# Sliding-window attention and SwiGLU on one Trainium2 core: a fence read moved from ScalarE to VectorE, and an eviction moved from VectorE to ScalarE

## The chip, the cores and the metric

The kernel runs on one core of a Trainium2 chip. Its time is the device time of one execution in microseconds. The core has five engines that run side by side, each with its own queue in program order: TensorE (PE in the profile; PEld is its weight loads), VectorE (DVE), ScalarE (ACT), GpSimd (POOL) and SyncE (SP, which issues DMAs). They wait for one another through semaphores.

## The reference

Causal attention with a window of 64 positions over 8 batches of 8 heads (576 positions, head size 64), then a gated feed-forward block over all 4608 tokens.

```python
scores = scale * np.matmul(q, k.transpose(0, 1, 3, 2))
rel = pos[:, None] - pos[None, :]
mask = (rel >= 0) & (rel < window)
...
attn = attn / (np.sum(attn, axis=-1, keepdims=True) + 1e-09)
return np.matmul(attn, v).astype(np.float32)
...
g = x @ w_gate
silu = g * (1.0 / (1.0 + np.exp(-g)))
val = x @ w_val
return (silu * val @ w_out).astype(np.float32)
```

The output of attention, as 4608 rows of 512, is `x`; `w_gate` and `w_val` are 512x1536, `w_out` is 1536x512.

## The kernel before

**Tiling.** The tokens go in nine steps, t = 0 to 8, of 512 tokens each: eight hold the first 512 positions of a batch, and step 7 (`LAST`) gathers the last 64 positions of all eight. The weights stay in SBUF as bf16. A step needs attention (scores, exponentials, masks, totals, mixing with v, division by the totals), the gate and value products with SiLU into `hT` (12 groups of 128 rows), and the projection with `w_out` into four groups of 128 tokens.

**Order.** The order of each engine's instructions is the order in which the program writes them; nothing reorders them. The loop over t from 1 (line 749) interleaves two steps: between the gate stage of step t-1 and that of step t, TensorE works on the attention of t and, between its pieces, on the projection of t-1. For t from 2 to 8 this stretch is, with line numbers of the kernel before:

1. `set_exp` (751): ScalarE loads the table with exp and ln. `scores(t, 0)` (752): 32 score matmuls in 64x64 quadrants of the array into the banks `two[0]` and `two[1]`, one for each h of two heads; then for each h an exponential on ScalarE (line 283) into `eb`, and on VectorE the product with the mask (286) and the sum `both` of two halves (291).
2. `project_quads(..., range(12), 0)` (753): the first half of the projection of token groups 0 and 2, in quadrants, into banks 5 and 7. The two row halves of the array (x = 0 and 1) work for different groups here, and swap groups in the second half.
3. The fence (754 to 757, and `marker(6, 1)` in 761). `marker` (367) is a matmul of 16 columns in one row half, into a bank that holds nothing. Two of them follow the first half of the projection, one in each row half. ScalarE reads one word of each of their banks into `seen`. A third marker, behind the scores of step 4, writes the second bank again and so waits for that read. Since TensorE's queue is in order, the second half of the projection starts behind it, and the two row halves cannot meet in one bank.
4. `scores(t, 1)` (760): the same as in 1 for the other two head pairs. Its matmuls write `two[0]` and `two[1]` again, so they wait for ScalarE's exponentials of step 1.
5. The second half of the quadrant projection (762, 764) with the totals of the first half of the heads between (`sums`, 763: matmuls of line 303, logarithms of line 317), then the mixing with v (766, line 381).
6. Group 0 is evicted by ScalarE (767); the totals of the other heads follow (768); `end()` inverts the totals by exp(-ln) on ScalarE (320). Group 2 is evicted by VectorE (771). Twelve matmuls project token group 1 into bank 5 (772, line 449).
7. `scale_all` (773): four products on VectorE (397) give `xT` of step t. `project_end(t - 1, 1, bank[5])` (774): VectorE copies group 1 from bank 5 to SBUF (line 469) and SP issues its four stores (488). Twelve matmuls project group 3 into bank 4 (775).
8. `set_silu` (776): ScalarE loads the SiLU table. VectorE evicts group 3 from bank 4 (778). POOL waits for `xT` with a one-column copy (779), casts v and issues loads for step t+2.
9. Twelve rounds of `gate_value` (794): eight matmuls (440) of 512 columns into a gate bank and a value bank, SiLU on ScalarE (433), product on VectorE (434). The gate bank alternates between banks 5 and 4 beginning with 5, the value bank between 7 and 6. Four rounds are followed by transposes of q and k of the next step on VectorE (208, 218).

Of the kernel before, what the change touches and what calls it, by code (L numbers as in the profile page):

```python
# [11 lines left out]
AF = mybir.ActivationFunctionType  # L12
# [5 lines left out]
def kernel(  # L18
# [10 lines left out]
    nc = tc.nc  # L29
    S, D, H = 576, 64, 8  # L30
# [15 lines left out]
    bank = [two[i][:, j] for i in range(2) for j in range(2)]  # L46
# [10 lines left out]
    eb = [cst.tile([P, 17, 64], BF16, name=f"eb{i}") for i in range(4)]  # L57
# [4 lines left out]
    seen = cst.tile([D, 1], FP32, name="seen")  # L62
# [3 lines left out]
    def batch(t):  # L66
        return t if t < LAST else t - 1

    def blocks(ap, t, lo, hi):

        e = 4 if t < TURNED else 16
        w = 64 // e
        return ap.rearrange("r (e x) -> r e x", e=e)[:, :, w * lo:w * hi]
# [176 lines left out]
    def half(x):  # L250
        return slice(64 * x, 64 * x + 64)

    def scores(t, w):

        qT = queries[t]
        s_ps = two[0], two[1]
        for j in range(8):
            if t == LAST:
                k_j = kT[t % 2 if j < 4 else 2]
                pieces = [(j, j + 1, 0, k_j, P * (j % 4) + 64),  # L260
                          (j, j + 1, 1, k_j, P * (j % 4))]
            else:
                pieces = [(j, min(8, j + 2), 0, kT[t % 2], 64 * j)]
            for lo, hi, c, src, k0 in pieces:
                for h in range(2):
                    for x in range(2):
                        slot = s_ps[h][half(x)].rearrange("r a b -> r (a b)")
                        n = hi - lo
                        o = P * j + 64 * c
                        nc.tensor.matmul(  # L270
                            slot[:, o:o + 64 * n].rearrange(
                                "r (n e y) -> r e n y", n=n, e=16
                            ),
                            src[half(h), 2 * w + x, k0:k0 + 64],
                            blocks(qT[half(h), 2 * w + x], t, lo, hi).rearrange(
                                "r e (n y) -> r e n y", n=n
                            ),
                        )
        n = 1024 if t == LAST else 960
        for h in range(2):  # L280
            E = eb[2 * w + h]
            flat = E[:].rearrange("r s z -> r (s z)")[:, 64:64 + n]
            nc.scalar.activation(  # L283
                flat, s_ps[h][:].rearrange("r a b -> r (a b)")[:, 0:n], AF.Exp, scale=0.125
            )
            nc.vector.tensor_mul(  # L286
                flat, flat, mask[:].rearrange("r j c e y -> r (j c e y)")[:, 0:n]
            )
            both = epool.tile([P, 8, 64], BF16, name="both", tag="both")
            lo = 2 if t == LAST else 0  # L290
            nc.vector.tensor_add(both[:], E[:, 1:17:2], E[:, lo:lo + 15:2])  # L291
            weights[t, w, h] = E, both

    def totals_first(u, d_ps):
        for h in range(2):
            nc.tensor.matmul(
                d_ps[half(h)], ones[:, 0:D], weights[0, u][:, h, :]
            )
# [71 lines left out]
    def mix(t, w, o):  # L370
        E = [weights[t, w, h][0] for h in range(2)]
        for j in range(8) if t == LAST else (0, 2, 4, 6, 1, 3, 5, 7):
            if t == LAST:
                pieces = [(j, j + 1, 2 * j + 1 + c, vl[:, j, 1 - c]) for c in range(2)]
            else:
                pieces = [(j, min(8, j + 2), 2 * j + 1, vb[t % 2][:, j])]
            for lo, hi, s0, src in pieces:
                n = hi - lo
                for h in range(2):
                    for x in range(2):  # L380
                        nc.tensor.matmul(  # L381
                            blocks(o[x][half(h)], t, lo, hi).rearrange(
                                "r e (n y) -> r n e y", n=n
                            ),
                            src[half(x), w, h],
                            E[h][half(x), s0:s0 + n].rearrange("r n (e y) -> r n e y", e=16),
                            start=lo == 0 and s0 == 1, stop=lo == 7 and (t != LAST or s0 == 16),
                        )
# [16 lines left out]
    def d_tile():  # L405
        return bank[6 + take("v")]
# [60 lines left out]
    def project_end(t, s, o_ps, copy=nc.vector.tensor_copy):  # L467
        os_ = fsb.tile([P, 512], FP32, name="os_", tag="os_", bufs=4)
        copy(os_[:], o_ps[:])
        rows = out[S * batch(t):S * batch(t) + 512]  # L470
        if t < TURNED or t == NT - 1:
            if t < TURNED:
                rows = rows.rearrange("(r e) f -> e r f", e=4)[s]
            else:
                rows = rows[P * s:P * s + P]
            if t < TURNED or s == 0:
                for i in range(2):
                    nc.sync.dma_start(rows[half(i)], os_[half(i)])
            else:
                nc.sync.dma_start(rows, os_[:])  # L480
            return
        if t == LAST:
            rows = out.rearrange("(b s) f -> b s f", s=S)[:, 512:S]
            rows = rows.rearrange("b (r e) f -> e b r f", e=16)
        else:
            rows = rows.rearrange("(r e) f -> e r f", e=16)
        for i in range(4):
            nc.sync.dma_start(rows[4 * s + i], os_[32 * i:32 * i + 32])

    def out_tile():  # L490
        return bank[4 + take("g")]
# [72 lines left out]
    on_v, on_p, on_a = nc.vector.tensor_copy, nc.gpsimd.tensor_copy, nc.scalar.copy  # L564
# [14 lines left out]
    def weigh_first(u):  # L579
        E = eb[u][:, 1:17].rearrange("r (h y) z -> r h (y z)", h=2)  # L580
        nc.scalar.activation(E, two[u % 2][:], AF.Exp, scale=0.125)
        weights[0, u] = E
# [134 lines left out]
    second_halves(1, hi, 0, on_v)  # L717
    for u in (2, 3):
        turn_q(1, u)
    scores(1, 0)  # L720
    tiles = [out_tile(), d_tile(), out_tile(), d_tile()]

    def columns(c0, c1, s0=0, s1=4):
        project_part(0, range(s0, s1), tiles[s0:s1], range(c0, c1))
# [1 line left out]
    columns(0, 2, 0, 2)  # L726
    columns(0, 2, 2, 4)
    columns(2, 3)
    scores(1, 1)
    columns(3, 7)  # L730
    ends = [sums(1, w, two[w:w + 1]) for w in range(2)]
    for end in ends:
# [16 lines left out]
    for t in range(1, NT):  # L749
        if t > 1:  # L750
            set_exp()
            scores(t, 0)
            project_quads(t - 1, tiles, range(12), 0)
            for x in range(2):
                marker(4 + 2 * x, x)
            for x in range(2):
                on_a(seen[:], bank[4 + 2 * x][0:D, 0:1])
            if t == 2:
                stage_v(3)
            scores(t, 1)  # L760
            marker(6, 1)
            project_quads(t - 1, tiles, range(7), 1)
            end = sums(t, 0, two[0:1])
            project_quads(t - 1, tiles, range(7, 12), 1)
            for w in range(2):
                mix_half(t, w, two[1 - w])
            project_end(t - 1, 0, tiles[0], on_a)
            ends = end, sums(t, 1, (bank[4], bank[6]))
            for end in ends:
                end()  # L770
            project_end(t - 1, 2, tiles[2])
            project_part(t - 1, (1,), (bank[5],), range(12))
            scale_all(t, (two[1], two[0]))
            project_end(t - 1, 1, bank[5])
            project_part(t - 1, (3,), (bank[4],), range(12))
        set_silu()
        if t > 1:
            project_end(t - 1, 3, bank[4], on_v)
        on_p(past[:], xT[t][:, 3, 0:1])  # L779
        if t + 1 == LAST:  # L780
            load_last_v()
        elif t + 1 < NT and t > 1:
            cast_v(t + 1)
        if t + 2 < NT:
            load_qk(t + 2)
            if t > 1 and t + 2 != LAST:
                stage_v(t + 2)
        if t == 2:
            k_l = cast.tile([P, 4, 4, 4 * D], BF16, name="k_l", tag="c0")
        if t in (2, 3):  # L790
            load_k(k_l, [(b, S - P) for b in range(4, 8)], quarters[2 * t - 4:2 * t - 2])
        turns = (6, 7, 9, 10) if t == 1 else (1, 4, 7, 10)
        for m in range(12):
            gate_value(t, m)
            if m in turns and t + 1 < NT:
                turn(t + 1, turns.index(m))
            if (t, m) in late:
                turn_k(kT[2], k_l, late.index((t, m)))
# [32 lines left out]
```

## Time and profile before

| | us |
|---|---|
| median of three runs | 324.82 |
| the three runs | 324.44, 324.82, 325.74 |
| the profiled execution | 324.94 |
| its span in the profile | 322.8 |
| granted TensorE clock | 0.999 |
| TensorE busy | 316.8 (98%) |
| VectorE busy | 213.4 (66%) |
| ScalarE busy | 168.8 (52%) |
| one step of the loop, t=5 (gate stage to gate stage) | 33.9 |

How to read it: times in the profile count from the span's start. A line of the timeline gives start, length, engine, source line, operation, output and inputs, how many like it were joined, and in brackets how long the engine had been idle and what ended that. The ends of matmuls are modelled: each is drawn longer than its distance to the next, so a row of matmuls overlaps. Rows of weight loads (PEld) have no such overlap, and their idle times show the distance. In a group's row stand busy time, mean length in ns, and the idle time ahead of its members with what ended it.

### The profile page before, as it was taken

The page shows a single profiled execution, that of the slowest core. Times are in us where ns is not written, and L with a number is a line of the kernel's source. Part 1 is how long each engine was busy: PE and PEld are TensorE (multiplying, and loading weights), DVE is VectorE, ACT ScalarE, POOL GpSimd, SP SyncE. Part 2 cuts the span into 40 slices and gives each one's busy share as a digit, 9 for nine tenths or more (in the row PEclk, how much of TensorE's full clock was granted, in tenths as well). Part 3 has the DMA queues.
Part 4 walks back from the last instruction along what each step waited for, and adds up shares of the span by engine and source line. Part 5 has one row for each costly group of instructions (what it writes and reads, how often), then busy time and mean ns, then how long its engine had stood idle before and what let it go on. Part 6 is the DMA issues. An engine that isn't in the chain of part 4 may idle for free.

```text
span 322.8 us, 8085 instructions
## 1 busy us (share of the span) xinstructions
PE 316.8 (98%) x3299; PEld 155.0 (48%) x3299; DVE 213.4 (66%) x342; ACT 168.8 (52%) x239; POOL 146.8 (45%) x267
## 2 busy tenths in 40 slices
PE   7999999999999999999999999999999999999996
PEld 4644444445444544454445544454446444544443
DVE  4856746497676856676588666867796576854422
ACT  5954665348533863376336823583347533863310
POOL 4955666777557235751751099407856300000000
PEclk9999999999999999999999999999999999999999
DMA  7999999999699449983996269619998400011003
GB/s 250 203 196 198 206 154 226 194 200 125 131 191 197 52 100 169 199 96 73 163 196 75 67 119 120 69 31 140 189 191 107 97 18 0 5 73 60 0 19 113
DMA packets 83525, 40.42 MB, mean 125 GB/s; under 512 B 64160, under 2 KB 78752, under 8 KB 83488
## 3 DMA queue, kind: packets, MB, share of 16 engines
q0 software_dynamic: 51488, 22.59, 58.0%
q1 hardware_dynamic: 31456, 16.79, 22.7%
q8 instruction: 26, 0.43, 0.6%
q10 hardware_dynamic: 544, 0.52, 0.5%
q14 instruction: 11, 0.09, 0.1%
HBM read 53.02 MB, written 9.44 MB: 194 GB/s over the span
## 4 chain that ended last, share of the span: by engine, by line
PE 78%; DMA 15%; POOL 3%; issue 2%; DVE 1%; SPq 0%; POOLq 0%
PE one L440 46%; PE one L449 14%; PE one L461 11%; DMA wv<-in_moe_w_val_dram 3%; DMA wo<-in_moe_w_out_dram 3%; DMA q_s<-in_q_dram 2%; PE two L270 2%; DMA wg<-in_moe_w_gate_dram 2%; PE two L381 2%; DMA k_s<-in_k_dram 1%; DMA q_f<-in_q_dram 1%; DMA vb<-in_v_dram 1%; POOL vb L153 1%; PE one L502 1%; POOL v L145 1%
## 5 line engine op out<-in xcount | busy, mean ns | idle before, releaser
L433 ACT ACTIVATE sg<-one 128x512 f32<-128x512 f32 x107 | 63.9, 597 | 123.5 <-PE one L440 97.5
L434 DVE TENSOR_TENSOR hT<-sg,one 128x512 bf16<-128x512 f32 x107 | 74.0, 692 | 63.5 <-PE one L440 59.4
L440 PE MATMUL one<-xT,wg 128*128 128x512 bf16 x416 | 106.7, 379 | 0.2
L440 PE MATMUL one<-xT,wv 128*128 128x512 bf16 x416 | 106.7, 379 | 0.1
L127 POOL DMA_DIRECT2D k_s<-in_k_dram x112 | 60.4, 564 | 28.8 <-DMA q_s<-in_q_dram 15.0
L440 PEld LDWEIGHTS <-wg 128*128 128x128 bf16 x416 | 40.5, 98 | 50.1 <-issue 2.1
L440 PEld LDWEIGHTS <-wv 128*128 128x128 bf16 x416 | 40.7, 98 | 49.4 <-issue 0.4
L449 PE MATMUL one<-wo,hT 128*128 128x512 bf16 x252 | 56.5, 379 | 0.0
L779 POOL COPY past<-xT 128x1 bf16<-128x1 bf16 x8 | 1.5, 190 | 89.8 <-DVE xT L397 89.8
L461 PE MATMUL one<-wo,hT 64*64 64x512 bf16 x672 | 40.0, 377 | 0.0
L449 PEld LDWEIGHTS <-hT 128*128 128x128 bf16 x252 | 23.8, 98 | 29.3 <-issue 2.0
L218 DVE STREAM_TRANSPOSE kT<-k_s 128x512 bf16<-128x512 bf16 x28 | 36.0, 1286 | 0.5 <-DMA vb<-in_v_dram 0.5
L397 DVE TENSOR_TENSOR xT<-two,r 128x512 bf16<-128x512 f32 x34 | 21.2, 683 | 22.1 <-ACT r L320 18.1
L283 ACT ACTIVATE eb<-two 128x960 bf16<-128x960 f32 (+1 forms) x32 | 29.5, 974 | 1.7 <-PE two L270 1.2
L286 DVE TENSOR_TENSOR eb<-eb,mask 128x960 bf16<-128x960 bf16 (+1 forms) x32 | 21.0, 656 | 7.0 <-ACT eb L283 6.8
L461 PEld LDWEIGHTS <-hT 64*64 64x64 bf16 x672 | 18.4, 107 | 14.5
L208 DVE STREAM_TRANSPOSE qT<-q_s 128x512 bf16<-128x512 bf16 x32 | 22.3, 701 | 0.1
L320 ACT ACTIVATE r<-r 128x1024 f32<-128x1024 f32 (+1 forms) x20 | 18.5, 972 | 0.1
L291 DVE TENSOR_TENSOR both<-eb 128x512 bf16<-128x512 bf16 x32 | 13.6, 425 | 1.1
L153 POOL DMA_DIRECT2D vb<-in_v_dram x16 | 10.9, 687 | 6.2 <-DMA wo<-in_moe_w_out_dram 3.7
L92 POOL DMA_DIRECT2D q_s<-in_q_dram x24 | 12.9, 546 | 1.2 <-DMA v<-in_v_dram 0.8
L510 ACT ACT_TABLE_LOAD x9 | 11.5, 1283 | 2.0 <-issue 1.9
(134 smaller groups left out, 241.1 us busy)
## 6 DMA issues: line engine op xcount, KB each, us to landing
k_s<-in_k_dram POOLq DMA_DIRECT2D x112, 56.0 KB, 5.3
q_s<-in_q_dram POOLq DMA_DIRECT2D x24, 248.0 KB, 6.7
v_f<-in_v_dram SPq DMA_DIRECT2D x40, 128.0 KB
wg<-in_moe_w_gate_dram POOLq DMA_DIRECT2D x5, 256.0 KB, 8.9
wv<-in_moe_w_val_dram POOLq DMA_DIRECT2D x5, 256.0 KB, 9.0
q_f<-in_q_dram SPq DMA_DIRECT2D x4, 256.0 KB
wo<-in_moe_w_out_dram POOLq DMA_DIRECT2D x2, 512.0 KB, 10.7
vb<-in_v_dram POOLq DMA_DIRECT2D x16, 64.0 KB, 6.5
```

The source lines that it names most:

```text
L127: nc.gpsimd.dma_start(k_s[p0:p0 + 32, g, :, 0:w], k[b, a:H:2, s:s + P].rearrange("u (r e) d -> r u (e d)", e=4) [:, :, 32 * c:32 * c + w],)
L208: nc.vector.transpose(queries[t][:, u, :].rearrange("r (e x) -> r e x", e=16), staged[t][0][:, u].rearrange("r (e d) -> r e d", d=D)[:, :, ...
L218: nc.vector.transpose(dst[:, u, :].rearrange("r (g x e) -> r g e x", g=4, e=4), k_s[:, :, u].rearrange("r g (e d) -> r g e d", d=D)[:, :, ...
L283: nc.scalar.activation(flat, s_ps[h][:].rearrange("r a b -> r (a b)")[:, 0:n], AF.Exp, scale=0.125)
L286: nc.vector.tensor_mul(flat, flat, mask[:].rearrange("r j c e y -> r (j c e y)")[:, 0:n])
L320: nc.scalar.activation(r, r, AF.Exp, scale=-1.0)
L397: nc.vector.tensor_mul(x, o_ps, r)
L433: nc.scalar.activation(sg[:], g_ps[:], AF.Silu)
L434: nc.vector.tensor_mul(hT[t][:, m, :], sg[:], v_ps[:])
L440: nc.tensor.matmul(ps[:], w[:, c, P * m:P * m + P], xT[t][:, c, :], start=(c == 0), stop=(c == 3),)
L449: nc.tensor.matmul(o_ps[:], hT[t][:, c, P * s:P * s + P], wo[:, c, :], start=(c == 0), stop=(c == 11),)
L461: nc.tensor.matmul(tiles[s][half(y)], hT[t][half(x), c, r0:r0 + 64], wo[half(x), c, :], start=not back and c == 0, stop=bool(back) and c = ...
```

## The change

`scores` no longer emits the masks itself. For each h it emits the exponential and returns a function that emits mask product and sum. Where nothing else changes (step 1, and the second call of each step) these functions are called at once, and VectorE and ScalarE keep their order. In the first call of each step from t=2 on, VectorE's order becomes: product and sum for h = 0, the two reads of the fence, product and sum for h = 1. The reads leave ScalarE. And `project_end` of token group 1 (line 774 before) copies with ScalarE, which puts the copy behind the inversions and ahead of the SiLU table load.

```diff
+        return [weigh(t, w, h, s_ps[h]) for h in range(2)]
+
+    def weigh(t, w, h, s_ps):
         n = 1024 if t == LAST else 960
-        for h in range(2):
-            E = eb[2 * w + h]
-            flat = E[:].rearrange("r s z -> r (s z)")[:, 64:64 + n]
-            nc.scalar.activation(
-                flat, s_ps[h][:].rearrange("r a b -> r (a b)")[:, 0:n], AF.Exp, scale=0.125
-            )
+        E = eb[2 * w + h]
+        flat = E[:].rearrange("r s z -> r (s z)")[:, 64:64 + n]
+        nc.scalar.activation(
+            flat, s_ps[:].rearrange("r a b -> r (a b)")[:, 0:n], AF.Exp, scale=0.125
+        )
+
+        def masked():
             nc.vector.tensor_mul(
                 flat, flat, mask[:].rearrange("r j c e y -> r (j c e y)")[:, 0:n]
             )
...
             weights[t, w, h] = E, both
+
+        return masked
+
+    def ready(masks):
+        for masked in masks:
+            masked()
...
-    scores(1, 0)
+    ready(scores(1, 0))
...
-    scores(1, 1)
+    ready(scores(1, 1))
...
             set_exp()
-            scores(t, 0)
+            masks = scores(t, 0)
+            masks[0]()
             project_quads(t - 1, tiles, range(12), 0)
             for x in range(2):
                 marker(4 + 2 * x, x)
             for x in range(2):
-                on_a(seen[:], bank[4 + 2 * x][0:D, 0:1])
+                on_v(seen[:], bank[4 + 2 * x][0:D, 0:1])
+            masks[1]()
             if t == 2:
                 stage_v(3)
-            scores(t, 1)
+            ready(scores(t, 1))
             marker(6, 1)
...
             scale_all(t, (two[1], two[0]))
-            project_end(t - 1, 1, bank[5])
+            project_end(t - 1, 1, bank[5], on_a)
             project_part(t - 1, (3,), (bank[4],), range(12))
```

## The prediction

> **What bounds the kernel now.** I read the page first: busy shares, then the chain that ended last.
>
> ```profile
> span 322.8 us, 8085 instructions
> ...
> PE 316.8 (98%) x3299; PEld 155.0 (48%) x3299; DVE 213.4 (66%) x342; ACT 168.8 (52%) x239; POOL 146.8 (45%) x267
> ...
> PE 78%; DMA 15%; POOL 3%; issue 2%; DVE 1%; SPq 0%; POOLq 0%
> ```
>
> TensorE (PE) is busy in 98% of the span and carries 78% of the chain; VectorE (DVE) and ScalarE (ACT) carry next to nothing. So an edit on DVE or ACT counts only where TensorE stands still for it. A busy PE hides short stops, because the drawn tail of one matmul covers the start of the next; I therefore looked for distances between matmul starts. The chain in order of time (start, length, what) shows two short pieces of "issue" in every step of the loop; those of step t=5 are:
>
> ```profile
> 176.74 0.01 issue
> 176.76 0.17 PE one L368
> ...
> 186.11 0.04 issue
> 186.14 20.88 PE one L440 x96
> ```
>
> They stand ahead of the fence's last matmul (line 368) and of the first gate matmul (line 440), the two places that the change touches. What holds TensorE there is read from the timeline (start, length, engine, group).
>
> First the entry into the gate stage: the pitch of undisturbed matmuls, the place itself in step t=5, then one row of step t=2 and the page's group of these weight loads.
>
> ```profile
> 153.12 1.03 PE L440 MATMUL one<-xT,wv 128*128 128x512 bf16 x4
> 153.98 1.03 PE L440 MATMUL one<-xT,wg 128*128 128x512 bf16 x4
> ...
> 184.81 0.68 DVE L397 TENSOR_TENSOR xT<-two,r 128x512 bf16<-128x512 f32 x1
> 185.41 0.68 DVE L469 COPY os__2849<-one 128x512 f32<-128x512 f32 x1
> 185.73 0.10 PEld L440 LDWEIGHTS <-wg 128*128 128x128 bf16 x1
> 186.14 0.38 PE L440 MATMUL one<-xT,wg 128*128 128x512 bf16 x1
> 186.15 0.69 DVE L469 COPY os__2868<-one 128x512 f32<-128x512 f32 x1
> ...
> 84.50 0.10 PEld L440 LDWEIGHTS <-wg 128*128 128x128 bf16 x1 [0.26 <-issue]
> ...
> L440 PEld LDWEIGHTS <-wg 128*128 128x128 bf16 x416 | 40.5, 98 | 50.1 <-issue 2.1
> ```
>
> Four matmuls take 153.98 - 153.12 = 0.86 us, so the pitch is 0.215. The first gate weights are loaded at 185.73, right behind the start of the last projection matmul, and the gate matmul should start at 185.73 + 0.215 = 185.945. It starts at 186.14. DVE's eviction of token group 1 ends at 185.41 + 0.68 = 186.09, just before. The first gate tile of a step is bank 5, the bank that this eviction reads, so TensorE waits for DVE: 0.195 us here. Between two loads an ordinary idle time is 0.215 - 0.098 = 0.117; step t=2 has 0.26, so it loses 0.145. The last row sums the idle time of the weight loader where nothing but the issue ended it, once in each of the seven steps: 2.1 - 7 x 0.117 = 1.28. Six times 0.195 and 0.145 give 1.31. I take 1.3 us.
>
> Now the fence of step t=5:
>
> ```profile
> 175.22 0.66 DVE L286 TENSOR_TENSOR eb<-eb,mask 128x960 bf16<-128x960 bf16 x1 [0.66 <-ACT eb L283]
> 175.92 0.42 DVE L291 TENSOR_TENSOR both<-eb 128x512 bf16<-128x512 bf16 x1
> 176.11 0.17 PE L368 MATMUL one<-ones 64*64 64x16 bf16 x2
> 176.11 0.63 PE L270 MATMUL two<-qT,kT 64*64 64x128 bf16 x32
> 176.26 0.65 DVE L286 TENSOR_TENSOR eb<-eb,mask 128x960 bf16<-128x960 bf16 x1
> 176.37 0.15 ACT L757 COPY seen<-one 64x1 f32<-64x1 f32 x1 [0.32 <-PE one L368]
> 176.55 0.15 ACT L757 COPY seen<-one 64x1 f32<-64x1 f32 x1
> 176.76 0.17 PE L368 MATMUL one<-ones 64*64 64x16 bf16 x1
> 176.78 1.83 ACT L283 ACTIVATE eb<-two 128x960 bf16<-128x960 f32 x2
> ```
>
> The two markers start at 176.11; ACT reads the first at 176.37 and the second from 176.55 to 176.70; the third marker follows at 176.76. The 32 score matmuls between them end at 176.74. They come four at a time, eight fours in 0.63 us including the tail of the last, which at the markers' 0.17 puts the last four near 176.55; TensorE could have gone on near 176.61. The fence costs about 0.15 us a step.
>
> **The change, part by part.** (1) *Group 1's eviction goes from DVE to ACT.* It leaves the path if ACT has it done before 185.9 and its table load is still in time.
>
> ```profile
> 181.86 2.00 ACT L320 ACTIVATE r<-r 128x1024 f32<-128x1024 f32 x2
> 182.92 0.59 PE L449 MATMUL one<-wo,hT 128*128 128x512 bf16 x2
> 183.88 1.28 ACT L513 ACT_TABLE_LOAD   x1
> 187.20 0.60 ACT L433 ACTIVATE sg<-one 128x512 f32<-128x512 f32 x1 [2.04 <-PE one L440]
> ...
> L469 ACT COPY os__2811<-one 128x512 f32<-128x512 f32 x1 | 0.6, 585 | 0.1
> ```
>
> Bank 5 is complete at 182.92 + 0.59 = 183.51 (these two are the last of its twelve matmuls); ACT's inversions end at 183.86. The copy then runs to about 184.45 (0.585 from the row of its twin, group 0), 1.4 us before the bank is wanted. The table load moves from 183.88 to about 184.47 and ends at 185.75. The first SiLU, now at 187.20, will be wanted 0.2 earlier, at 187.00: 1.25 us of cover, and a late SiLU would still hold TensorE only at the third gate tile, which takes its bank again 16 matmuls or 3.4 us behind the first. So the load costs nothing; only with all of that gone would the copy's 0.585 a step, 4.1 in seven, come back. Next in line for the gate matmul are the four scalings: the last ends at 184.81 + 0.68 = 185.49, 0.4 before it is needed, and stays. DVE's other eviction, at 186.15, waits for the last projection matmul (185.73, and its 0.38) and stays too. The four stores of the evicted tile keep their place on SP's queue, behind those of group 2; nothing on SP or POOL is moved past another. Gain: 1.3.
>
> (2) *The two fence reads go from ACT to DVE, between the masks of the two heads.* No row shows such a pair on DVE. The nearest are a single read in the first stage, its marker, and the copy behind it:
>
> ```profile
> 12.66 0.17 PE L368 MATMUL one<-ones 64*64 64x16 bf16 x1
> ...
> 12.88 0.15 DVE L654 COPY seen<-one 64x1 f32<-64x1 f32 x1 [0.24 <-PE one L368]
> 13.05 0.35 DVE L655 COPY mask<-v 64x512 bf16<-64x512 bf16 x1
> ```
>
> One read takes 0.15 on either engine. On ACT the second starts 0.18 after the first, 0.03 after its end: both write one word. DVE shows the same distance where an operation depends on the one before it: 175.22 + 0.66 = 175.88, next 175.92. So the pair takes 0.34 on either. DVE can begin when it is free: the second mask product started at 176.26, and the marker is there at 176.37. DVE is 0.11 early, and the fence opens within 0.01 of where it did. The last step has the same cover (278.65 against 278.76, below). Only t=2 differs, where DVE is behind:
>
> ```profile
> 74.61 0.43 DVE L291 TENSOR_TENSOR both<-eb 128x512 bf16<-128x512 bf16 x1
> 74.78 0.34 ACT L757 COPY seen<-one 64x1 f32<-64x1 f32 x2 [0.31 <-PE one L368]
> 74.95 0.65 DVE L286 TENSOR_TENSOR eb<-eb,mask 128x960 bf16<-128x960 bf16 x1
> ...
> 278.65 0.65 DVE L286 TENSOR_TENSOR eb<-eb,mask 128x960 bf16<-128x960 bf16 x1
> 278.76 0.34 ACT L757 COPY seen<-one 64x1 f32<-64x1 f32 x2 [0.32 <-PE one L368]
> ```
>
> There DVE is free at 74.95, 0.17 after ACT's read: 0.17 more on TensorE, once. Bounds for the fence: at best its whole wait goes, 7 x 0.15 = 1.05 gained. At worst each read costs what DVE's copy at 13.05 does, 0.35, so the pair 0.70 for 0.34: 7 x 0.36 + 0.17 = 2.7 lost. I take the value of the single read's row, which is the same instruction: 6 x 0.01 + 0.17 = 0.2 lost.
>
> The Trainium skill ("VectorE: DVE Perf Modes", The DRAIN you can't avoid) says that the next operation does not start until the pipe is empty, though one that is not held may start earlier. With the first half of that, the reads would begin at the end of the sum before them: 176.34, still ahead of 176.37, but 75.04 for 74.95 in t=2, and the loss would be 0.3 for 0.2. The row at 176.26 starts 0.08 before that end, so the trace bears out the second half.
>
> (3) *Behind the reads* on DVE stand the second head's mask product and sum, then the masks of the second half; the totals (line 303) wait for that sum.
>
> ```profile
> 177.78 0.66 DVE L286 TENSOR_TENSOR eb<-eb,mask 128x960 bf16<-128x960 bf16 x1 [0.41 <-ACT eb L283]
> 178.08 0.12 PEld L303 LDWEIGHTS <-ones 64*64 64x64 bf16 x4
> ```
>
> The product slips from 176.26 to at most 176.74, and its sum, which ended 0.69 + 0.42 after its start, to 177.85. The totals' weights load at 178.08, 0.2 later; the next mask idled 0.41 for ACT and slips by a few hundredths at most. With this cover gone every further tenth would show at line 303, 0.7 us in seven steps. ACT has 0.34 less to do, but its exponentials at 176.78 wait for the scores' end at 176.74, so that gains nothing. In step t=1 each engine keeps its order.
>
> **Sum.** -1.3 + 0.2 = -1.1 us. The profiled execution took 324.94 (span 322.8 and 2.1 around it), so 323.8; the median of the runs, 324.82, lies 0.12 below it. I predict 323.7, 0.3% faster.
>
> **Rivals.** *The fence shortens too*, because DVE's two reads overlap, as its independent operations do by 0.08, or the marker reaches DVE sooner: the pair shrinks by up to 0.12, 7 x 0.12 = 0.8 more, 322.9, at the bound 322.5. For it: the lone read started 0.22 after its marker (12.66 to 12.88) against 0.26 here (176.11 to 176.37). Against: the word that both write. *No gain at the gate*, because another release stands right behind the eviction's: only t=2's 0.17 is left, 325.0. Against: the scalings, the next one, are 0.4 early. *The fence becomes longer than the gate stall was.* All of it lies at line 368: TensorE stands behind the pair, so from a pair of 0.34 + 1.1/7 = 0.50 on the gain is used up, and at 0.70 the time is 324.82 - 1.3 + 2.7 = 326.2, and every further 0.05 adds 0.35. For it: DVE has never run such a pair here. Against: its single read is 0.15.
>
> **How the numbers follow.** Forecast 0.63 (323.2 to 324.2, its own range, half the fence's gain either way), shorter fence 0.18, no gain 0.10, longer fence 0.09. The range takes in the shorter fence and the lost gain and leaves the longer fence out: 322.8 to 325.0. A measurement of this kernel tells 0.5%, 1.6 us, from no change. Faster than 323.2 is most of the second case and an edge of the first: 0.19. Slower than 326.4 is the upper part of the last: 0.06. The rest, 0.75, is within.
>
> **What would show it.** Right: in all seven steps the first gate matmul starts 0.215 behind its weight load, and the loader's idle time falls from 2.1 to about 0.8; an ACT copy of 0.585 stands ahead of each line 513 load; the reads on DVE are 0.18 apart, the third marker 0.65 behind the first, 0.17 more in t=2. Wrong: a third marker closer than 0.6 (shorter fence) or beyond 0.8 (longer); a wait for DVE at line 303; a gate distance that stays near 0.41.

## The result, and the profile after

The changed kernel takes 324.15 us in the median (323.57 to 325.08, 20 runs) against 324.97 for the kernel before in 20 runs (324.4 to 325.77). The ratio is 0.9975, with a 95% interval of 0.9965 to 0.9984: 0.8 us faster. The interval leaves out a ratio of 1, although single runs of the two kernels overlap; the gain is smaller than the 0.5% that the prediction said a measurement can tell from no change. Forecast was a gain of 1.1 us.

The page of the changed kernel, and the group of the gate's weight loads (idle time is the number behind the second bar):

```profile
span 322.1 us, 8061 instructions
...
PE 95%; DMA 1%; DVE 1%; issue 1%; ACT 1%; DVEq 0%
...
L450 PEld LDWEIGHTS <-wg 128*128 128x128 bf16 x416 | 40.5, 98 | 48.9
```

Line 450 is line 440 of the kernel before. The 2.1 us of idle time that "issue" ended is gone from the row; the prediction had left 0.8 of it as ordinary idle time, which the row does not put down to "issue". The entry into the gate stage of step t=5, in the timeline:

```profile
183.72 0.59 ACT L479 COPY os__2849<-one 128x512 f32<-128x512 f32 x1
184.33 1.28 ACT L523 ACT_TABLE_LOAD   x1
186.98 0.60 ACT L443 ACTIVATE sg<-one 128x512 f32<-128x512 f32 x1 [1.37 <-PE one L450]
...
185.48 0.60 PE L459 MATMUL one<-wo,hT 128*128 128x512 bf16 x2
185.70 0.31 PEld L450 LDWEIGHTS <-wg 128*128 128x128 bf16 x2
185.92 0.38 PE L450 MATMUL one<-xT,wg 128*128 128x512 bf16 x1
```

Weight load at 185.70, gate matmul at 185.92: the ordinary pitch, where it was 0.41. The copy ends at 184.31, the table load at 185.61, and the first SiLU waits for its matmuls for 1.37 us, not for the table. Over all seven steps the distance between the last projection matmul and the first gate matmul is 0.215 to 0.217, against 0.354 to 0.414 before.

The fence of the same step; "seen" is now VectorE's:

```profile
175.82 0.42 DVE L295 TENSOR_TENSOR both<-eb 128x512 bf16<-128x512 bf16 x1
176.01 0.17 PE L378 MATMUL one<-ones 64*64 64x16 bf16 x2
176.27 0.15 DVE L768 COPY seen<-one 64x1 f32<-64x1 f32 x1
176.52 0.15 DVE L768 COPY seen<-one 64x1 f32<-64x1 f32 x1
176.60 0.64 DVE L290 TENSOR_TENSOR eb<-eb,mask 128x960 bf16<-128x960 bf16 x1
176.73 0.17 PE L378 MATMUL one<-ones 64*64 64x16 bf16 x1
177.28 0.42 DVE L295 TENSOR_TENSOR both<-eb 128x512 bf16<-128x512 bf16 x1
177.68 0.66 DVE L290 TENSOR_TENSOR eb<-eb,mask 128x960 bf16<-128x960 bf16 x1
178.05 0.12 PEld L313 LDWEIGHTS <-ones 64*64 64x64 bf16 x4
```

The first read begins 0.26 us behind the first marker, as on ScalarE. The second begins 0.25 behind the first, where ScalarE took 0.18. The third marker stands 0.715 behind the first; it stood 0.645 before. So TensorE waits 0.07 us longer, and the traces show the same in every one of the seven steps. What lies behind the reads is covered: the second head's sum ends at 177.70, the totals' weights load at 178.05.

### The profile page after: what moved, and what is told of

It is laid out like the page before. It is cut to its first block, busy times and chain, and to the rows that moved or that the text cites. A ratio compares the mean times of both kernels' runs of the same rounds, so it can differ in the third digit from the quotient of the medians.

```text
span 322.1 us, 8061 instructions
## 1 busy us (share of the span) xinstructions
PE 314.7 (98%) x3269; PEld 155.4 (48%) x3299; DVE 210.9 (65%) x349; ACT 170.0 (53%) x232; POOL 146.9 (46%) x267
## 4 chain that ended last, share of the span: by engine, by line
PE 95%; DMA 1%; DVE 1%; issue 1%; ACT 1%; DVEq 0%
PE one L450 56%; PE one L459 17%; PE one L471 11%; PE two L391 2%; PE two L270 2%; PE one L426 2%; DMA q_f<-in_q_dram 1%; PE two L313 1%; PE one L512 1%; PE one L196 1%; DVE seen L768 1%; PE two L426 1%; PE one L378 0%; PE one L313 0%; PE two L715 0%
## 5 line engine op out<-in xcount | busy, mean ns | idle before, releaser
L450 PE MATMUL one<-xT,wg 128*128 128x512 bf16 x406 | 104.8, 379 | 0.1
L459 PE MATMUL one<-wo,hT 128*128 128x512 bf16 x241 | 55.7, 380 | 0.7 <-issue 0.2
L407 DVE TENSOR_TENSOR xT<-two,r 128x512 bf16<-128x512 f32 x34 | 21.3, 684 | 22.3 <-ACT r L330 18.3
L208 DVE STREAM_TRANSPOSE qT<-q_s 128x512 bf16<-128x512 bf16 x32 | 22.3, 700 | 0.1
```

Source lines behind the costliest of these rows:

```text
L208: nc.vector.transpose(queries[t][:, u, :].rearrange("r (e x) -> r e x", e=16), staged[t][0][:, u].rearrange("r (e d) -> r e d", d=D)[:, :, ...
L407: nc.vector.tensor_mul(x, o_ps, r)
L450: nc.tensor.matmul(ps[:], w[:, c, P * m:P * m + P], xT[t][:, c, :], start=(c == 0), stop=(c == 3),)
L459: nc.tensor.matmul(o_ps[:], hT[t][:, c, P * s:P * s + P], wo[:, c, :], start=(c == 0), stop=(c == 11),)
```

## The experiments

Each kernel ran beside the kernel before on one chip, though not all on the same chip, so kernels are compared by their ratios to it (with 95% intervals) and not by their medians. Because the time of one execution also moves with its start (last section), the table has beside the ratio three distances from the trace of each kernel: first to third marker, last projection matmul to first gate matmul (both in step t=5), and the period from one step's first gate matmul to the next's (t=4 to t=5).

| kernel | ratio | median, us | third marker | gate | period |
|---|---|---|---|---|---|
| before | 1 | 324.97 | 0.645 | 0.414 | 33.88 |
| changed | 0.9975 (0.9965 to 0.9984) | 324.15 | 0.715 | 0.216 | 33.76 |
| eviction alone | 0.9949 (0.9931 to 0.9968) | 322.94 | 0.645 | 0.216 | 33.69 |
| fence alone | 1.0004 (0.9992 to 1.0016) | 324.92 | 0.715 | 0.415 | 33.95 |
| two words, VectorE | 0.9935 (0.9916 to 0.9953) | 322.55 | 0.527 | 0.216 | 33.57 |
| two words, ScalarE | 0.9923 (0.9905 to 0.9941) | 322.14 | 0.523 | 0.216 | 33.56 |
| third read, VectorE | 0.9996 (0.9983 to 1.0009) | 324.82 | 0.899 | 0.216 | 33.94 |
| copy behind the load | 0.9973 (0.9961 to 0.9985) | 324.16 | 0.715 | 0.216 | 33.75 |
| one read, VectorE | 0.9907 (0.989 to 0.9923) | 322.07 | 0.470 | 0.216 | 33.50 |
| one read, ScalarE | 0.9910 (0.9894 to 0.9926) | 322.11 | 0.465 | 0.216 | 33.50 |
| reads behind both masks | 1.0183 (1.0153 to 1.0213) | 330.80 | 1.63 | 0.216 | 34.67 |
| reads ahead of both masks | 1.0092 (1.0077 to 1.0107) | 327.65 | 0.719 | 0.216 | 34.29 |

**The two parts apart.** From the kernel before:

```diff
-            project_end(t - 1, 1, bank[5])
+            project_end(t - 1, 1, bank[5], on_a)
```

> The kernel before with one edit: group 1 is evicted by ScalarE ahead of its table load; the fence stays on ScalarE. Theory (the changed kernel gains 1.3 us at the gate and gives 0.5 back at the fence): the first gate matmul follows the last projection matmul by 0.216 us in all seven steps (0.35 to 0.41 before), third marker 0.645 us behind the first as before, time 1.3 us below before, ratio 0.996. Rival (the gain at the gate needs VectorE's reads elsewhere, or part of the gain is the fence's): a smaller gain than the changed kernel's 0.8 us.

And from the changed kernel the same line back:

```diff
-            project_end(t - 1, 1, bank[5], on_a)
+            project_end(t - 1, 1, bank[5])
```

> The changed kernel with group 1 evicted by VectorE again: only the fence reads are moved. Theory: third marker 0.71 us behind the first instead of 0.645, gate distance 0.41 as before, so 7 x 0.07 = 0.5 us slower than before, ratio 1.0015. Rival (the fence on VectorE is worth something by freeing ScalarE): ratio 1.000 or below.

The weight loads of the eviction alone, then of the fence alone:

```profile
L440 PEld LDWEIGHTS <-wg 128*128 128x128 bf16 x416 | 40.5, 98 | 48.8
```

```profile
L450 PEld LDWEIGHTS <-wg 128*128 128x128 bf16 x416 | 40.5, 98 | 50.1 <-issue 2.2
```

The wait at the gate goes and comes with the eviction, whatever engine reads the fence; the 0.07 us at the fence goes and comes with the reads. The periods add up: the eviction alone is 0.19 below before, the fence alone 0.07 above it, both together 0.12 below. The fence alone can't be told from no change by its ratio; it is the period and the marker that show its cost. The rival that moving the reads has a worth of its own fell by them too; the ratio would have left it open. The eviction alone was faster than expected (0.9949 for 0.996), though its interval holds 0.996. Its profiled execution has a span 1.65 us shorter than that of before: 1.30 at the gates, 0.28 because the load of v that came late before (below) did not, and the rest in the mixing of step 7.

**Why the pair of reads is longer on VectorE.** The program waits in two places for the second read: for its marker, and for the first read, since both write the same word. The changed kernel's group of the reads:

```profile
L768 DVE COPY seen<-one x14: 149/150/151, 75.0 to 278.4; 64x1 f32<-64x1 f32 x14
L768 DVEq EVENT_SEMAPHORE  x7: 21/21/21, 75.2 to 278.4; - x7
```

There is one separate wait event of 21 ns in each step, in VectorE's queue between the reads. ScalarE had one in each step as well, in the kernel before:

```profile
L757 ACTq EVENT_SEMAPHORE  x7: 38/38/38, 74.8 to 278.8; - x7
```

But the two stand at different places. In all seven steps ScalarE's event began 0.006 us behind the start of the first read and was over 0.1 us before that read ended; the second read started 0.03 behind that end. VectorE's event begins 0.04 behind the end of the first read, so it is the wait for that read, and the second read starts another 0.04 behind the event. A word for each read should take VectorE's event away:

```diff
-    seen = cst.tile([D, 1], FP32, name="seen")
+    seen = [cst.tile([D, 1], FP32, name=f"seen{x}") for x in range(2)]
...
-                on_v(seen[:], bank[4 + 2 * x][0:D, 0:1])
+                on_v(seen[x][:], bank[4 + 2 * x][0:D, 0:1])
```

> The changed kernel, with a word of its own for each of the two fence reads on VectorE, so that the second doesn't wait for the first. Theory (the fence is 0.07 us longer on VectorE because the second read needs two waits, the own-engine one standing alone in the queue for 21 ns and adding 0.1 us behind the first read): no wait event between the reads, the second starts 0.07 to 0.11 behind the first, third marker 0.53 to 0.57 behind the first instead of 0.715, 7 x 0.16 = 1.1 us below the changed kernel, ratio to before 0.994. Rival (VectorE is simply slower in taking up a marker, or in releasing TensorE): third marker stays at 0.70 or more.

> The kernel before with group 1 evicted by ScalarE, and the fence on ScalarE with a word of its own for each read. Theory (it is the shared word, not the engine): the second read starts 0.05 to 0.1 behind the first instead of 0.185, third marker 0.53 to 0.57 behind the first, ratio to before 0.994, the same as two words on VectorE. Rival (the reads are better on VectorE): ratio 0.996, as with the eviction alone.

Two words on VectorE, then two words on ScalarE (with the eviction on ScalarE in both):

```profile
175.74 0.17 PE L378 MATMUL one<-ones 64*64 64x16 bf16 x1
...
176.00 0.22 DVE L768 COPY seen<-one 64x1 f32<-64x1 f32 x2
176.14 0.64 DVE L290 TENSOR_TENSOR eb<-eb,mask 128x960 bf16<-128x960 bf16 x1
...
176.27 0.17 PE L378 MATMUL one<-ones 64*64 64x16 bf16 x1
```

```profile
174.94 0.17 PE L368 MATMUL one<-ones 64*64 64x16 bf16 x1
...
175.19 0.21 ACT L757 COPY seen<-one 64x1 f32<-64x1 f32 x2 [0.31 <-PE one L368]
...
175.46 0.17 PE L368 MATMUL one<-ones 64*64 64x16 bf16 x1
```

The pair takes 0.22 us on VectorE and 0.21 on ScalarE, and the periods are 33.57 and 33.56. So neither the taking up of a marker nor the release of TensorE is slower on VectorE; what made the difference was the wait that the shared word brings. Both kernels beat the changed one.

**The cost of one read more.** The first marker's bank is read twice, so there are three reads into one word:

```diff
-            for x in range(2):
+            for x in (0, 0, 1):
                 on_v(seen[:], bank[4 + 2 * x][0:D, 0:1])
```

> The changed kernel with one more read of the first marker's bank into the same word, so three dependent reads in the fence. Theory (TensorE stands behind the reads one for one, and a dependent read on VectorE costs 0.25 us): third marker 0.97 us behind the first instead of 0.715, step period 34.01 instead of 33.755, 7 x 0.253 = 1.8 us above the changed kernel, ratio to before 1.003. Rival (the fence is covered by the scores, so its length matters only in part): less than 1 us more, ratio below 1.001.

```profile
176.06 0.17 PE L378 MATMUL one<-ones 64*64 64x16 bf16 x1
...
176.32 0.15 DVE L768 COPY seen<-one 64x1 f32<-64x1 f32 x1
176.50 0.15 DVE L768 COPY seen<-one 64x1 f32<-64x1 f32 x1
176.76 0.15 DVE L768 COPY seen<-one 64x1 f32<-64x1 f32 x1
...
176.96 0.17 PE L378 MATMUL one<-ones 64*64 64x16 bf16 x1 [0.27 <-DVE seen L768]
```

A miss in size, and a useful one. The third marker came 0.184 later than in the changed kernel, not 0.25, and the period grew by the same 0.18. In this trace the second read, of the marker already seen, starts 0.184 behind the first; the third, of the other marker, 0.255 behind the second. So a read that waits for its forerunner alone costs 0.184 on VectorE, just what it cost on ScalarE; 0.07 more come only where it waits for a marker too; the trace has its one wait event ahead of the third read and none ahead of the second. One for one, the part of the theory that was at stake, held in the period: what the reads grew by, the period grew by. The whole time does not show it. The ratio of 0.9996 lies below the 1.001 that the rival (the fence matters only in part) had named, and the period alone would give about 1.001. The span of this trace is 0.85 longer than the changed kernel's: 1.29 at the fences, and 0.50 less because the first gate matmul of step 0 started earlier (21.83 against 22.33); the rest is the mixing of step 7. Whether the other runs differ by their starts in the same way is not shown; the rival is answered by the period alone.

**Where the copy stands to the table load.** The copy is moved behind the load:

```diff
         set_silu()
         if t > 1:
+            project_end(t - 1, 1, bank[5], on_a)
             project_end(t - 1, 3, bank[4], on_v)
```

> The changed kernel with ScalarE's copy of group 1 behind the SiLU table load instead of ahead of it. Theory (the copy only has to end before the last projection matmul does, and there are 1.4 us to spare ahead of the load, so about 0.15 to 0.2 us behind it): gate distance stays 0.216, step period 33.755, ratio to before 0.9975. Rival (the place ahead of the load is what the gain rests on): gate distance above 0.3 and the 1.3 us gone, ratio 1.001.

```profile
183.32 1.28 ACT L523 ACT_TABLE_LOAD   x1
184.62 0.59 ACT L479 COPY os__2862<-one 128x512 f32<-128x512 f32 x1
186.44 0.60 ACT L443 ACTIVATE sg<-one 128x512 f32<-128x512 f32 x1 [1.24 <-PE one L450]
...
185.38 0.38 PE L450 MATMUL one<-xT,wg 128*128 128x512 bf16 x1
```

The copy ends at 185.21, 0.17 us ahead of the gate matmul at 185.38, and nothing changes. The gain rests on the engine, not on the place ahead of the load. The copy starts 0.01 us behind the load's end.

**One read.** The read of the first marker is left out on VectorE (from the changed kernel), and on ScalarE (from the kernel before, with the eviction on ScalarE):

```diff
-            for x in range(2):
-                on_v(seen[:], bank[4 + 2 * x][0:D, 0:1])
+            on_v(seen[:], bank[6][0:D, 0:1])
```

> The changed kernel without the read of the first marker: only the second marker's bank is read, on VectorE. Theory: third marker at 0.26 + 0.15 + 0.05 = 0.46 us behind the first, where the scores' own end (0.43 to 0.45) takes over, so 0.47 to 0.49; step period 33.53; ratio to before 0.9925. Rival (the marker reaches an engine only at a fixed distance of some 0.5 us, or the first read stands for something else): third marker at 0.53 or more, as with two words.

> The kernel before with group 1 evicted by ScalarE, and one read of the second marker's bank on ScalarE as the whole fence. Theory (the engine of the read makes no difference): third marker 0.47 to 0.49 us behind the first, step period 33.52 to 33.54, ratio to before 0.992. Rival (moving the reads to VectorE was worth something of itself): a longer period than with one read on VectorE.

One read on VectorE:

```profile
174.73 0.17 PE L378 MATMUL one<-ones 64*64 64x16 bf16 x1
...
174.97 0.15 DVE L767 COPY seen<-one 64x1 f32<-64x1 f32 x1
...
175.20 0.17 PE L378 MATMUL one<-ones 64*64 64x16 bf16 x1
```

The read is over at 175.12, before the scores are, and the third marker follows the last score matmul by 0.03 us where it stood 0.2 (before) or 0.27 (changed) behind it. The fence costs nothing any more on either engine: period 33.50, ratios 0.9907 and 0.9910. By the period these are the fastest of the kernels; by the ratios the kernels with two words can't be told from them (overlapping intervals). The fence then rests on the second marker not finishing ahead of the first; that order was not tested by itself.

**Where the reads stand among the masks.** Behind both, and ahead of both:

```diff
+            masks[1]()
             for x in range(2):
                 on_v(seen[:], bank[4 + 2 * x][0:D, 0:1])
-            masks[1]()
```

> The changed kernel with the two reads behind both of the first masks instead of between them. Theory (TensorE stands behind VectorE's reads one for one, wherever VectorE gets to them): the reads begin about 1.2 us behind the first marker instead of 0.26, the third marker stands 1.65 to 1.75 behind the first, step period 34.70 instead of 33.755, 6.6 us above the changed kernel, ratio to before 1.018. Rival (the scores and exponentials of the second half cover part of it): ratio below 1.010.

```profile
180.49 0.42 DVE L295 TENSOR_TENSOR both<-eb 128x512 bf16<-128x512 bf16 x1
180.84 0.40 DVE L769 COPY seen<-one 64x1 f32<-64x1 f32 x2
181.29 0.17 PE L378 MATMUL one<-ones 64*64 64x16 bf16 x1 [1.00 <-DVE seen L769]
```

As expected, within 0.03 us of period, with the third marker just ahead of the expected 1.65: TensorE idles a whole microsecond there for VectorE. The pair takes 0.40 here too, though its reads start 1.18 us behind the markers, so the 0.07 us is not a late second marker.

```diff
             masks = scores(t, 0)
-            masks[0]()
...
-            masks[1]()
+            ready(masks)
```

> The changed kernel with the two reads ahead of both of the first masks. Theory (the fence opens as before, but VectorE now idles until the markers and the masks come 1 us late, past the 0.2 us of cover at the totals): third marker at 0.715 us behind the first, totals' first matmul 2.28 instead of 1.54 behind the third marker, step period 34.5, 5.2 us above the changed kernel, ratio to before 1.014. Rival (the masks have more cover than was read off the trace): ratio below 1.005.

```profile
178.22 0.64 DVE L290 TENSOR_TENSOR eb<-eb,mask 128x960 bf16<-128x960 bf16 x1
178.90 0.43 DVE L295 TENSOR_TENSOR both<-eb 128x512 bf16<-128x512 bf16 x1
179.24 0.65 DVE L290 TENSOR_TENSOR eb<-eb,mask 128x960 bf16<-128x960 bf16 x1
179.93 0.43 DVE L295 TENSOR_TENSOR both<-eb 128x512 bf16<-128x512 bf16 x1
```

```profile
179.89 0.92 PE L313 MATMUL two<-both,ones 64*64 64x512 bf16 x4
180.41 1.48 PE L471 MATMUL one<-wo,hT 64*64 64x512 bf16 x20
```

The size and the place were off. The totals' first matmul kept its distance, 1.54 behind the third marker, because it needs only the first head's sum (ended at 179.33); the second head's sum ends at 180.36, and the four totals, drawn in 0.39 us elsewhere, stretch over 0.92. The step loses 0.53 us, not 0.75: the cover behind the reads is larger than was read off the trace, since it must be counted to the second pair of totals.

## Why the prediction was right, and what was mis-sized

*The wait at the gate* was right in cause and size. 1.31 us were worked out; seven gate distances of 0.216 in place of 0.354 to 0.414 give 1.30. The scalings, the next in line, were indeed early, the table had its cover, and the eviction alone gave the same distances.

*The fence* had the right mechanism and the wrong size. The prediction said "the pair takes 0.34 on either" and counted 6 x 0.01 + 0.17 = 0.2 us lost. The pair took 0.40, and 7 x 0.07 = 0.5 us were lost. The step that failed is the transfer of ScalarE's 0.03 us between dependent reads to VectorE. The row of VectorE used for it, mask product to sum, is an operation with one wait, and the second read has two. The three-read kernel shows both in one step: 0.184 with one wait, 0.255 with two. ScalarE's second read also had a wait event ahead of it, but one that was over before the first read ended. That this place of the event is what makes the engines differ is read from the times; no run changed it alone. With that term put right the sum is -1.3 + 0.5 = -0.8 us, and 0.8 is what was measured. That it meets so closely is partly luck: the interval runs from 0.5 to 1.1 us, and the two parts measured alone, -1.7 and +0.1 by their ratios, do not add up to -0.8. It is the periods that add up.

*The fence's whole wait*, taken as 0.15 us a step for the best case, was a little larger: with one read the third marker came 0.175 earlier than before, and the period was 0.19 shorter than with the eviction alone.

*The 0.17 us of step t=2* did not appear. In the changed kernel's trace the read follows its marker there as everywhere:

```profile
74.56 0.43 DVE L295 TENSOR_TENSOR both<-eb 128x512 bf16<-128x512 bf16 x1
...
74.75 0.17 PE L378 MATMUL one<-ones 64*64 64x16 bf16 x1
...
75.00 0.40 DVE L768 COPY seen<-one 64x1 f32<-64x1 f32 x2
```

VectorE's lateness is in the profile of before alone; none of the eleven other traces has it. Only one execution of the kernel before was traced, so whether its other runs have it is open. Its chain runs through a load of v that ended at 64.59 and held a transpose of VectorE for 0.5 us; the changed kernel's list of waits has no such row. The two rows of before, a piece of the chain and the wait:

```profile
60.93 3.66 DMA vb<-in_v_dram
```

```profile
DVE kT L218 <- DMA vb<-in_v_dram: 0.5, 1, 0.5
```

*What lies behind the reads* (totals and later masks) was covered as said, even with a pair 0.07 longer.

*Rivals.* "The fence shortens too" did not happen in the changed kernel, because of the word that both reads write, the objection named there; two words make it happen (0.527). "No gain at the gate" and "the fence becomes longer than the gate stall was" fell; the reads behind both masks show how TensorE pays for a fence 0.9 us longer, and it costs 1.8%.

*The profiled executions* differ by 0.7 us of span, and the trace splits it: -1.30 at the gates, +0.49 at the fences, -0.28 for the late load of the execution before, -0.12 in the mixing of step 7, and +0.50 because the first gate matmul of step 0 started later (22.33 against 21.84).

## What to carry to other kernels

Where one engine is busy throughout, look for distances between its starts that are longer than the pitch, and ask which release came last at each; both stops of this kernel were invisible in the busy share. A fence should do as little as possible: reads that only serve as fence need no word in common, and one of them may do, as long as the second marker cannot finish ahead of the first (not tested here). That was worth more than the choice of the engine (0.19 us a step on ScalarE and 0.26 on VectorE, against 0.07). On VectorE an instruction with two waits cost more than one with a single wait, so a cost taken from a row should come from the same engine and from an instruction with the same waits: the number was the same on ScalarE, and the cost was not.

## What was not expected of the hardware

A second wait on a VectorE instruction appeared as an event of its own, 21 ns long, and set the instruction back by 0.07 us, where ScalarE's event of 38 ns ran while the first read was still under way, and its second read started 0.03 behind the first one's end.

The first microseconds differ from execution to execution. The 32 transposes of the start take 220 ns in the mean in the profile of before and 243 in that of the changed kernel, and both kernels with one read have 243:

```profile
L196 PE MATMUL one<-identb,qk_b 128*128 128x128 bf16 x32 | 2.5, 220 | 0.4 <-ACT qk_b L567 0.4
```

```profile
L196 PE MATMUL one<-identb,qk_b 128*128 128x128 bf16 x32 | 2.9, 243 | 0.4 <-ACT qk_b L577 0.4
```

The first gate matmul of step 0 started at 21.8 us in some traces and at 22.3 to 23.2 in others, with either engine at the fence. A mean of 243 goes with 21.8 (one read on VectorE) as well as with 22.6 (one read on ScalarE), so the transposes alone do not decide it. The mixing of step 7 differs as well, from 1.14 to 1.84 us over the twelve traces. Changes of 0.2% are better read from the period of the steps between, which repeats within 0.01 us, than from single executions. What decides the start was not tested.
